# Two transposes of Wq issued ahead of the transpose of tile 7's normalised rows

## The chip, the cores and the metric

The kernel runs on one core of one Trainium2 chip. The metric is device time in microseconds (us), as a median of runs; one further execution is recorded by the hardware profiler, and all times inside the kernel are counted from the start of that record's span.

## What is computed

The reference is one transformer layer on 2048 rows of 640 numbers in bf16: linear attention with 32 heads of 20 features, whose feature map is a pair of softmaxes, and then a feed-forward part with silu.

```python
qkv = layernorm(x) @ wqkv                     # to q, k, v, each 32 heads x 20
pq, pk = q @ w_phi, k @ w_phi                 # per head, 20 x 20
phi_q = concat(softmax(pq), softmax(-pq))     # 40 features; phi_k likewise
kv = phi_k^T @ v;  z = sum_s(phi_k)           # per head
o = (phi_q @ kv) / (phi_q . z + 1e-6)
h = x + o @ wo
out = h + silu(layernorm(h) @ w1) @ w2
```

## The kernel before

The 2048 rows are 16 tiles of 128 rows. The small matrices w_phi are folded into the weights first: Wfk is Wk times w_phi, Wfq is Wq times w_phi, so that each tile is projected straight onto the arguments of the softmaxes. Matmuls contract over the partitions, in five chunks of 128.

**One list sets the order.** Every step of the program has a short name, and the list `ORDER` (lines 18 to 55) writes them out in the order in which their instructions are emitted. Each engine carries out its own instructions in that order; only semaphores hold it against the other engines. A step that only issues DMAs is an instruction of SyncE (SP), which has its own queue and takes its issues strictly in turn: an issue that waits for its data holds all the issues behind it.

The names that matter here, with t for a tile and r for one of six blocks of Wq:

- `st`t, `rs`t, `xn`t: mean and variance of tile t (VectorE, L432 and L433), one over the deviation (L441 and L444 on GpSimd, or L438 and L439 on ScalarE), and the normalised rows (L448; on GpSimd for most tiles from 3 on). `xn` has four buffers.
- `xt`t: the transpose of the normalised rows into XnT. From tile 4 on it is a DMA transpose issued by SyncE (L477). It reads what `xn`t has written.
- `K`t, `V`t: the projections of tile t onto keys and values, ten matmuls each (L496), with XnT as the stationary operand. `Q`t is the same for queries (L534).
- `wq`r: block r of the columns of Wq, 120 wide, read from DRAM and transposed into WTq by a DMA transpose on SyncE (L386). It waits for no other step.
- `fq`r, `fq`r`e`: five matmuls that fold block r (L398), and ScalarE's copy of the result into Wfq (L404). The blocks are folded in the order 2, 3, 0, 1, 4, 5. `Q0` needs all six.
- `ex`t, `su`t, `rk`t, `sc`t: the exponentials of tile t's keys (ScalarE, L551), their sums (VectorE, L555), the inverse of the sums (ScalarE, L563 and L564) and the scaling (VectorE, L568). `kv`t are the eleven matmuls that add the tile to the sum over all rows (L587), and `ve`t copies the values out of PSUM (L572).
- `load`i: a load of a later weight (L488), issued by SyncE. `load6` brings the first three chunks of w2.
- Later: `D`, `E`, `ot`, `G` for the attention's second half, `hn`, `ht` for the second normalisation and its transposes to HnT (L769), `u` and `d` for the feed-forward part (L824, L864).

PSUM is used in three pairs of banks, taken in turn: `fq0`, `K6`, `fq1`, `K7`, `V6`, `fq4` and so on, each pair to be read out before its next use.

The two lines that issue the transposes in question are these:

```python
nc.sync.dma_start_transpose(WTq[:, r : r + 1, :], A_wqkv[:, at : at + P])      # wq, L386
nc.sync.dma_start_transpose(xt(t), xn_.pop(t)[:])                              # xt, L477
```

Of the kernel before, what the change touches and what calls it, by code (L numbers as in the profile page):

```python
# [22 lines left out]
rs4 xt2 K1 ex0 V0.2 ones5 xn4 wq4 V0.3 V0.1 st5 x2 wph0 su0 ex1 su1 rs5 V0.4 K2 xn5 phq xt3 V1 rs6 ex2  # L23
V2 x3 st7 xn6 rk0 X8 su2 rs7 ve1 ve2 ve0 xt4 sc0 st8 V3 fq2 xt5 rk2 ve3 K3 xn7 st11 ones3 fq2e V4 K4 rk1
ex3 wq3 ones2 ve4 kv0 ones6 sc1 ones7 sc2 V5 fq3 rs8 st9 ex4 su3 st10 rs9 wq0 kv1 ve5 ones4 xt6 su4 K5
fq0 fq3e K6 rk3 ex5 xt7 kv2 wq1 wq5 fq1 fq0e sc3 ex6 K7 load6 su5 fq1e mask kv3 ex7 xn8 st13 V6 xt8
mask0 rk4 ve6 rk5 su6 sc4 rs11 fq4 fq4e xn9 zeros st12 V7 ve7 rk6 V8 rs10 sc5 xt9 xn10 load3 V9 su7 ve8
fq5 rs12 rs13 st14 ve9 xt10 kv4 fq5e rk7 load7 K8 ex8 sc6 kv5 st15 xn11 K9 su8 xn12 sc7 Q0 kv6 K10 xt11
kv7 ex9 Q1 rk8 rs15 load2 su9 xn13 qe0 ex10 qe1 K11 xt13 sc8 rs14 mask1 rk9 qs0 kv8 xt12 xn14 load11 V10
# [911 lines left out]
```

## Time and profile before

| | |
|---|---|
| median of three runs | 237.27 us (236.63 to 237.54) |
| the profiled execution's own time | 236.82 us |
| its span | 234.8 us |
| TensorE (PE) busy | 229.5 us, 98% of the span |
| VectorE (DVE) busy | 165.8 us, 71% |
| ScalarE (ACT) busy | 105.1 us, 45% |
| GpSimd (POOL) busy | 64.4 us, 27% |
| granted TensorE clock | 0.999 |

The profile has a page with sums by engine and by line, and the trace behind it can be asked for stretches of time: a timeline by engine (start, duration, what ran), who waited for whom (total, times, longest), and the chain of work that ended last (start, duration, what). DMA transposes appear in SyncE's rows with the time that their issue takes; the time to landing is told beside them. Names such as `XnT<-xn` say what is written from what.

### The profile page before, as it was taken

How to read it: one execution, taken by the hardware profiler on the slowest of the kernel's cores; microseconds unless marked ns; L12 is line 12 of the kernel's file. 1: busy time of each engine (PE TensorE's matmuls, PEld its weight loads, DVE VectorE, ACT ScalarE, POOL GpSimd, SP SyncE). 2: the span in 40 equal slices, each digit the busy share in tenths (PEclk: the TensorE clock that was granted, in tenths of full speed). 3: DMA queues.
4: the chain of work that ended last, by engine and by line, in shares of the span. 5: the costliest groups of instructions: out<-in, count | busy, mean ns of one | idle time of the engine just before them, and what ended most of it. 6: DMA issues, size and time to landing. Idle time of an engine off the chain costs nothing.

```text
span 234.8 us, 5031 instructions
## 1 busy us (share of the span) xinstructions
PE 229.5 (98%) x1984; PEld 161.2 (69%) x1984; DVE 165.8 (71%) x349; ACT 105.1 (45%) x222; POOL 64.4 (27%) x103
## 2 busy tenths in 40 slices
PE   8999989999999999999999999999999999999995
PEld 6777767777777777887545777645677455778874
DVE  3999979999999999999999795792472330404031
ACT  3999979877969754610234100054300326001410
POOL 5699999996000020121010111011020010100000
PEclk9999999999999999999999999999999999999999
DMA  6995379668976749694325946127313301011011
GB/s 165 346 228 138 88 162 149 181 59 172 245 270 73 155 94 159 148 120 95 81 64 133 163 97 173 31 56 176 72 24 88 98 0 28 30 29 56 8 56 56
DMA packets 67213, 26.79 MB, mean 114 GB/s; under 512 B 60151, under 2 KB 66167, under 8 KB 67063
## 3 DMA queue, kind: packets, MB, share of 16 engines
q1 hardware_dynamic: 66535, 26.47, 52.9%
q8 instruction: 15, 0.25, 0.5%
q10 hardware_dynamic: 656, 0.03, 0.2%
q14 instruction: 7, 0.06, 0.1%
HBM read 9.64 MB, written 2.62 MB: 52 GB/s over the span
## 4 chain that ended last, share of the span: by engine, by line
PE 87%; DVE 5%; DMA 3%; ACT 2%; issue 1%; POOL 1%; SPq 0%; DVEq 0%; POOLq 0%
PE banks L864 24%; PE banks L824 24%; PE banks L496 16%; PE banks L742 7%; PE banks L534 4%; PE banks L587 2%; PE banks L215 2%; PE banks L867 2%; PE banks L709 2%; DMA HnT<-xn 2%; DMA WTq<-in_A_wqkv_dram 1%; DVE Sq L660 1%; ACT Wfk L323 1%; PE banks L835 1%; DVE O L722 1%
## 5 line engine op out<-in xcount | busy, mean ns | idle before, releaser
L844 ACT ACTIVATE shT<-banks 128x512 bf16<-128x512 f32 (+1 forms) x53 | 28.7, 591 | 83.2 <-PE banks L824 83.2
L864 PE MATMUL banks<-w_sb,shT 128*128 128x320 bf16 (+2 forms) x429 | 61.3, 295 | 0.0
L824 PE MATMUL banks<-HnT,w_sb 128*128 128x512 bf16 (+1 forms) x325 | 59.0, 336 | 0.5 <-DMA HnT<-xn 0.5
L864 PEld LDWEIGHTS <-shT 128*128 128x128 bf16 x429 | 41.1, 98 | 15.2
L824 PEld LDWEIGHTS <-w_sb 128*128 128x128 bf16 x325 | 31.1, 98 | 22.8 <-issue 0.6
L441 POOL TENSOR_SCALAR rs<-mv 128x1 f32<-128x1 f32 x26 | 7.7, 298 | 137.1 <-DVE mv L433 136.9
L873 DVE TENSOR_TENSOR o_t<-banks,X 128x320 bf16<-128x320 f32 (+2 forms) x33 | 14.9, 474 | 39.6 <-PE banks L867 26.7
L496 PEld LDWEIGHTS <-XnT 128*128 128x128 bf16 x300 | 28.2, 98 | 10.5 <-DMA XnT<-xn 0.4
L448 POOL TENSOR_SCALAR xn<-X,mv,rs 128x640 bf16<-128x640 bf16 x12 | 31.0, 2586 | 0.4
L432 DVE BATCH_NORM_STATS2 st<-X 128x6 f32<-128x320 bf16 x64 | 27.9, 477 | 3.3 <-DMA X<-in_A_x_dram 3.2
L656 ACT ACTIVATE EQ<-banks 128x360 bf16<-128x360 f32 (+2 forms) x52 | 22.0, 514 | 8.4 <-PE banks L534 8.2
L742 PE MATMUL banks<-wo_sb,OT 128*128 128x320 bf16 x160 | 24.8, 299 | 0.0
L660 DVE TENSOR_REDUCE Sq<-EQ 128x66 f32<-128x1320 bf16 x16 | 24.1, 1517 | 0.0
L534 PE MATMUL banks<-Wfq,XnT 128*128 128x360 bf16 (+2 forms) x160 | 23.5, 299 | 0.0
L749 DVE TENSOR_TENSOR X<-banks,X 128x320 bf16<-128x320 f32 x32 | 14.5, 483 | 12.6 <-PE banks L742 12.5
L555 DVE TENSOR_REDUCE Sk<-EK 128x64 f32<-128x1280 bf16 x16 | 23.3, 1464 | 0.2
L551 ACT ACTIVATE EK<-banks 128x640 bf16<-128x640 f32 x32 | 20.8, 701 | 4.4 <-PE banks L496 2.0
L496 PE MATMUL banks<-Wfk,XnT 128*128 128x320 bf16 x150 | 22.5, 299 | 0.0
L496 PE MATMUL banks<-Wv,XnT 128*128 128x320 bf16 x150 | 21.8, 299 | 0.0
L742 PEld LDWEIGHTS <-OT 128*128 128x128 bf16 x160 | 15.1, 98 | 6.5
L534 PEld LDWEIGHTS <-XnT 128*128 128x128 bf16 x160 | 15.1, 97 | 6.2
L444 POOL TENSOR_TENSOR rs<-rs,nhalf_t 128x1 f32<-128x1 f32 x26 | 15.9, 613 | 2.2
(71 smaller groups left out, 203.9 us busy)
## 6 DMA issues: line engine op xcount, KB each, us to landing
out_dram<-o_t SPq DMA_DIRECT2D x15, 160.0 KB, 2.0
w_sb<-in_B_w_dram SPq DMA_DIRECT2D x5, 432.0 KB, 3.9
w_sb<-in_B_w_dram SPq DMA_DIRECT2D x3, 480.0 KB, 4.5
X<-in_A_x_dram SPq DMA_DIRECT2D x1, 1280.0 KB, 7.3
Wk<-in_A_wqkv_dram SPq DMA_DIRECT2D x5, 160.0 KB, 3.5
Wv<-in_A_wqkv_dram SPq DMA_DIRECT2D x5, 160.0 KB, 5.7
wo_sb<-in_A_wo_dram SPq DMA_DIRECT2D x1, 800.0 KB, 5.7
X<-in_A_x_dram SPq DMA_DIRECT2D x1, 640.0 KB, 5.9
```

Source lines behind the costliest of these rows:

```text
L432: nc.vector.bn_stats(st[:, i, :], X[:, t, i * HD : (i + 1) * HD])
L448: eng.tensor_scalar(out=xn_[t][:], in0=X[:, t, :], scalar1=mv_.pop(t)[:, 0:1], scalar2=rs_.pop(t)[:], op0=ALU.subtract, op1=ALU.mult,)
L496: nc.tensor.matmul(ps[:, g, 0:HD], XnT[:, c, t * P : (t + 1) * P], W[:, c, g * HD : (g + 1) * HD], start=(c == 0), stop=(c == C - 1),)
L534: nc.tensor.matmul(ps[:, 0 : e - a], XnT[:, c, t * P : (t + 1) * P], Wfq[:, c, a:e], start=(c == 0), stop=(c == C - 1),)
L551: nc.scalar.activation(E5[:, :, :, b, :], p4, AF.Exp, scale=sign)
L555: nc.vector.tensor_reduce(sk[t][:], ek[t][:, 0 : H * HF].rearrange("p (q f) -> p q f", f=DH), axis=AX.X, op=ALU.add)
L656: nc.scalar.activation(features(t, a, b)[:, :, :, i], p4, AF.Exp, scale=sign)
L660: nc.vector.tensor_reduce(sq[t][:], EQ[0][:, t, :, 0:FCH].rearrange("p c (q f) -> p c q f", f=DH), axis=AX.X, op=ALU.add)
L742: nc.tensor.matmul(ps[:, 0:HD], ot[t][:, c, :], wo_sb[:, c, g * HD : (g + 1) * HD], start=(c == 0), stop=(c == C - 1),)
L824: nc.tensor.matmul(ps[:, at : at + n], w1_sb[:, c, fc * P : fc * P + P], HnT[u][:, c, 0:n], start=(c == 0), stop=(c == C - 1),)
L844: nc.scalar.activation(shT[u][:, f0 * n : f1 * n], ps_of.pop(("u", u, f0))[:, 0 : (f1 - f0) * n], AF.Silu)
L864: nc.tensor.matmul(ps[:, 0 : b - a], shT[u][:, at : at + P], w2_sb[:, fc, a:b], start=(fc == 0), stop=False,)
```

## The change

Two names of the list move: `wq1` and `wq5` stand ahead of `xt7` and `kv2`, in place of behind them.

```diff
-fq0 fq3e K6 rk3 ex5 xt7 kv2 wq1 wq5 fq1 fq0e sc3 ex6 K7 load6 su5 fq1e mask kv3 ex7 xn8 st13 V6 xt8
+fq0 fq3e K6 rk3 ex5 wq1 wq5 xt7 kv2 fq1 fq0e sc3 ex6 K7 load6 su5 fq1e mask kv3 ex7 xn8 st13 V6 xt8
```

`xt7`, `wq1` and `wq5` are issues of SyncE; `kv2` belongs to PE. SyncE's issues in this stretch were xt6, xt7, wq1, wq5, load6, xt8, and are now xt6, wq1, wq5, xt7, load6, xt8. The instructions of the other four engines, and their order, are the same as before.

## The prediction

> **What bounds the kernel now.** The page comes first: PE is busy 229.5 of 234.8 us, so at most 5.3 us are to be had, and a saving counts only where PE stands still. The chain of waits from 28 to 36.6 us then shows the place that the change touches.
>
> ```profile
> 28.51 2.91 DMA WTq<-in_A_wqkv_dram
> 31.42 0.05 issue
> 31.47 0.44 PE banks L398 x5
> 31.90 1.36 PE banks L496 x10
> ```
>
> The fold of query block 1 (fq1, five matmuls, L398) starts when the second block of Wq (wq1, L386) has landed, 2.91 us after its issue. The waits between 24 and 44 us give the price, and what hangs on it:
>
> ```profile
> DVE EK L568 <- ACT Rk L564: 1.7, 1, 1.7
> ...
> PE banks L398 <- DMA WTq<-in_A_wqkv_dram: 1.0, 1, 1.0
> ```
>
> PE is idle 1.04 us (30.43 to 31.47). K7 behind it is late by as much, so are ex7 and rk4 on ACT, and DVE stands 1.67 us before sc4 (L568, 35.45). From there DVE has no gap over 0.2 us until 110. The only other PE gap over 0.1 us after 11 us is 0.52 us before L824 at 92.73. SyncE's timeline says why wq1 is late:
>
> ```profile
> 23.48 4.98 SPq L477 DMA_TRANSPOSE XnT<-xn  x2
> 28.51 2.58 SPq L386 DMA_TRANSPOSE WTq<-in_A_wqkv_dram  x2
> 31.14 0.58 SPq L488 DMA_DIRECT2D w_sb<-in_B_w_dram  x1
> 31.82 3.45 SPq L477 DMA_TRANSPOSE XnT<-xn  x2
> ```
>
> The first row holds xt6 (23.48 to 24.70) and xt7 (27.25 to 28.46). Between them SyncE stands 2.55 us, until GpSimd has written xn7 (24.70 + 2.52 = 27.22), and wq1 and wq5 queue behind it though their data lie in DRAM.
>
> **The change part by part.** Nothing is added or removed. Three issues change places on SyncE; kv2, also named in the moved stretch, is PE's and keeps its place there.
>
> (1) *wq1 and wq5, earlier.* An issue takes 1.26 us and the next follows 0.05 later: wq1 24.75 to 26.01, wq5 26.06 to 27.32. The six wq took 2.9 to 6.4 us to land, wq1 itself 2.91: it lands near 27.7, at 29.0 with the 4.3 us of xt6 ahead of it. fq1 is ready for it at 30.43. The wait goes: **-1.04 us** at fq1, with 1.4 us of cover.
>
> (2) *xt7, moved past.* It issues at 27.37 in place of 27.25 and landed 3.5 us after issue, at 30.76; now 30.87 or so. K7 is the next on PE and, without the wait, is ready at 30.43 + 0.43 = 30.86. So xt7 is next late, by 0 to 0.1: I take 0.06, and keep **-0.97**. Bounds from the twelve xt: the fastest (2.4 us) lands before 30 and costs nothing; xt6, which also followed two wq at once, took 4.3: 31.63, and K7 is where it was. I take xt7's own row.
>
> (3) *Moved with it.* load6 (480 KB) issues at 28.6, not 31.14. xt8 stood behind it; it now waits for xn8 alone (GpSimd, 30.86), issues 0.9 us earlier and lands by 35.7 (issue end 32.1 plus the 3.5 it took before). V8 comes at 36.58 - 0.97 = 35.61: nothing lost. xt9 still goes at 34.05 and landed at 37.06, V9 wants it at 37.0: nothing to 0.1.
>
> (4) *The earlier PE then meets GpSimd.* GpSimd works without a break from 10.9 to 54 us, and each xt goes when its xn is done. V13 is the close one: xt13 issued at 47.88 and landed at 50.30 (2.4 us); V13 started at 50.86, the second ten of these thirty:
>
> ```profile
> 49.34 4.24 PE L496 MATMUL banks<-Wv,XnT 128*128 128x320 bf16 x30
> ```
>
> With PE 0.97 earlier V13 wants it at 49.89. GpSimd gains something: its small steps are long where they start while DVE runs an L568.
>
> ```profile
> 44.03 0.23 POOL L441 TENSOR_SCALAR rs<-mv 128x1 f32<-128x1 f32 x1
> 44.35 1.00 POOL L444 TENSOR_TENSOR rs<-rs,nhalf_t 128x1 f32<-128x1 f32 x1
> 45.35 2.51 POOL L448 TENSOR_SCALAR xn<-X,mv,rs 128x640 bf16<-128x640 bf16 x1
> ```
>
> That L444 started inside the L568 at 44.11 to 44.92 and took 1.00, not the usual 0.57; the L441 at 37.53 took 0.89, not 0.24. With DVE 0.97 earlier both stand clear: 0.43 + 0.65 saved, less up to 0.45 where xn10 now starts inside sc4, and 0.06 to 0.3 where xn12 and rs13 meet sc7. I take 0.37 to 0.56, so xn13 ends near 47.4, and xt13 would land near 49.85: in time. From 64 us DVE hangs on PE again (0.13 us of idle before su15, for ex15), so the 0.97 reaches the HnT gap at 92.73 and the end.
>
> The Trainium skill's page "SBUF — State Buffer", section "SBUF: two separate sides", calls the port pair of VectorE and GpSimd an exclusive lock held by whichever starts first. The rows above agree (1.00 against 0.57); without that rule xt13 would land at 50.30 as before, and the saving would end at 0.45.
>
> (5) *But a transfer of another kind goes by PE's clock.* Queue q8 moves 16 KB of instructions at a time, and each comes after some 250 more PE instructions in the trace (217, 432, 684, 946 before the first four), so it will be as much earlier as PE. The DMA view from 50.1 to 50.3 shows the fourth (start 50.19, 1.70 us long), and in the same answer the xt12 issued beside it:
>
> ```profile
> q8 instruction: 1, 0.02, 53.1%
> ...
> XnT<-xn SPq DMA_TRANSPOSE x1, 4.3
> ```
>
> xt12 took 4.3 us instead of 2.4. The second fetch (25.35, 1.23 us) fell on the last packets of xt6: 15 of its 16 completions came by 26.05, the last at 27.75, 1.17 us after the fetch ended. In before, xt13's last packets started at 49.85, so the fetch missed it by 0.34 us. Now PE, and the fetch with it, is 0.97 earlier and xt13 only 0.37 to 0.56: the fetch moves 0.41 to 0.60 towards it, and falls on its last packets. Price: fetch at 49.22, over at 50.50 (1.28, the two others of 1.23 and 1.28 before 40 us), xt13 complete 1.17 later at 51.67, V13 at 51.72 where it was at 50.86: **+0.86 us** against before. Bounds: a fetch of 1.23 and a completion 0.55 after it, as the undisturbed ones have, give +0.2; 1.70 long gives +1.28. If the fetch misses, -0.97.
>
> The fetches are also where the skill speaks against my sum: "Runtime: NRT & Kernel Launch", section "Instruction fetch mechanics", says that the cost of crossing a 16 KiB boundary is mostly hidden. By it the sum would stay at -0.97. xt12's 4.3 us, against 2.4, is why I weigh it lower: the fetch may cost the engine that it feeds nothing, and still hold up a transfer of another queue.
>
> K12 behind it has xt12 in time in either case (52.5, wanted after 52.9), and nothing later takes the +0.86 back: ex12 and su12 had 0.17 us of room, and DVE then reaches su15 by PE's clock.
>
> *Sum:* -1.04 at fq1, +0.07 for xt7, +1.83 at V13 = +0.86. The profiled execution took 236.82 (span 234.8 and 2.0 around it), so 237.68 by it. The median of before is 237.27, 0.45 above that execution; set on the median, **238.1**.
>
> **The rivals.**
> - *The gain is carried through*: the fetch misses xt13. For it: the margin that decides is 0.1 us of last packets, and one engine of sixteen carries the fetch. -0.97, 236.3; with less of the 0.52 at 92.73, 235.9.
> - *Half is kept*: xt7 lands some tenths later, or GpSimd gains nothing and V13 waits for an xt13 that lands at 50.30 undisturbed. PE is then at most 0.5 early. -0.45, 236.8.
> - *Slower at once*: K7 waits for xt7 behind wq5. The point from which it decides is a landing after 31.7. For it: the xt6 row (4.3 us behind two wq); against it: SyncE's issues are as far apart (1.3) as the wq landings (1.5), so no backlog should build. At 4.3 us there is nothing left to gain (237.3); at 2.4 us behind a wq5 that lands at 31 it is 33.4, +1.6: 238.9.
>
> That the change doesn't do what it says is excluded: only SyncE's order differs between the two programs.
>
> **How the numbers follow.** Fetch on xt13: 0.44 (half of it above +1.18, with a long fetch or more of xt13 caught). Carried through: 0.30 (0.16 of it beyond -1.18, since the three runs scatter by 0.9 and the 92.73 gap can shrink). Half kept: 0.12. xt7 late: 0.14 (0.08 above +1.18). 0.5% is 1.19 us, about what a measurement of this kernel can tell from no change: faster 0.16, same 0.54, slower 0.30. The likeliest case alone spans 237.5 to 238.6; with the gains and the late xt7, 235.9 to 238.9.
>
> **What would show it.** Right: no gap before fq1; K7 near 30.9; xn13 done before 47.6; a q8 transfer near 49.2 with xt13 landing after 51; a PE gap of 1 to 2 us before V13. Wrong: xt13 landing before 50 with no gap (then the end is 0.9 to 1.0 earlier), or K7 behind its old 31.74. The forecast fails if the fetches do not move with PE, or if a fetch leaves a transfer that is all but done alone.

## The result and the profile after

The changed kernel takes 238.61 us (median of 22 runs, 236.86 to 239.31) against 237.28 us before (22 runs, 236.63 to 238.43). The ratio is 1.0043, with a 95% interval of 1.0027 to 1.0059: 1.0 us slower (0.6 to 1.4). The two medians alone lie 1.33 us apart. Of the 22 runs of each kernel, 17 lie above 237.9 us after the change and 3 before it.

The profiled execution took 239.23 us (span 237.2, where before's was 234.8). SyncE's timeline has the new order:

```profile
23.91 1.22 SPq L477 DMA_TRANSPOSE XnT<-xn  x1
25.18 3.38 SPq L386 DMA_TRANSPOSE WTq<-in_A_wqkv_dram  x2
28.65 1.22 SPq L477 DMA_TRANSPOSE XnT<-xn  x1
29.92 0.58 SPq L488 DMA_DIRECT2D w_sb<-in_B_w_dram  x1
31.33 1.22 SPq L477 DMA_TRANSPOSE XnT<-xn  x1
```

The rows are xt6, wq1 and wq5 together, xt7, load6, xt8. wq1 is early, but the pair takes 3.38 us and not 2.58, so xt7 goes at 28.65. This execution was about 0.4 us behind before's already where the two programs do not differ (xt6 at 23.91 against 23.48); beyond that xt7 is 1.0 us later.

PE's timeline around the two places where it now stands still (the bracket is the idle time before the row and what ended it):

```profile
30.66 0.42 PE L398 MATMUL banks<-phi_q,WTq 128*128 128x120 bf16 x5
32.28 1.53 PE L496 MATMUL banks<-Wfk,XnT 128*128 128x320 bf16 x10 [1.19 <-DMA XnT<-xn]
...
49.67 1.52 PE L496 MATMUL banks<-Wv,XnT 128*128 128x320 bf16 x10
52.60 2.62 PE L496 MATMUL banks<-Wv,XnT 128*128 128x320 bf16 x18 [1.41 <-DMA XnT<-xn]
```

fq1 (L398) waits no more. K7 right behind it waits 1.19 us for xt7: the 1.04 us before fq1 have changed their name. The second gap is new: V13 waits 1.41 us for xt13. The chain of waits goes back through that transfer to GpSimd:

```profile
44.48 0.88 POOL rs L441
45.36 0.07 issue
45.43 0.57 POOL rs L444
46.00 2.50 POOL xn L448
48.50 0.03 POOL rs L441
48.53 4.02 DMA XnT<-xn
52.55 0.05 issue
52.60 0.45 PE banks L496 x2
```

Before, xt13 landed 2.42 us after its issue; here it took 4.02. Its 16 completions came at 50.79 to 50.95 for fifteen of them and at 52.55 for the last. The DMA view of the stretch from 50.4 to 50.6 shows what started there:

```profile
q8 instruction: 1, 0.02, 29.1%
q1 hardware_dynamic: 27, 0.00, 7.2%
```

This is PE's instruction fetch of 16 KB (start 50.51), and the 27 small packets are the last of xt13.

The difference of 2.4 us between the two spans can be followed by the times at which PE starts the same matmul: 0.4 at the start (gaps at 5 to 10 us, on loads that the change does not touch), 0.15 at fq1 and K7 together, 0.2 won back at V8 (which in before started at 36.62 for an xt8 that landed at 36.58), 1.57 at V13 (1.41 of it counted as idle, because PE's rows overlap), and 0.5 more in the gap before L824 (1.02 against 0.52).

### The profile page after: what moved, and what is told of

Its sections match the earlier page's. It is cut to its first block, busy times and chain, and to the rows that moved or that the text cites. A ratio compares the mean times of both kernels' runs of the same rounds, so it can differ in the third digit from the quotient of the medians.

```text
span 237.2 us, 5031 instructions
## 1 busy us (share of the span) xinstructions
PE 229.0 (97%) x1984; PEld 160.5 (68%) x1984; DVE 165.9 (70%) x349; ACT 104.9 (44%) x222; POOL 64.7 (27%) x103
## 4 chain that ended last, share of the span: by engine, by line
PE 69%; POOL 13%; DVE 6%; DMA 5%; issue 5%; SPq 1%; POOLq 0%; DVEq 0%
PE banks L864 24%; PE banks L824 24%; POOL xn L448 8%; PE banks L742 7%; PE banks L496 5%; PE banks L534 3%; PE banks L867 2%; DMA Wk<-in_A_wqkv_dram 2%; DMA XnT<-xn 2%; PE banks L709 2%; POOL rs L444 2%; DMA HnT<-xn 1%; POOL rs L441 1%; DVE Sq L660 1%; PE banks L587 1%
## 5 line engine op out<-in xcount | busy, mean ns | idle before, releaser
L824 PE MATMUL banks<-HnT,w_sb 128*128 128x512 bf16 (+1 forms) x325 | 59.0, 336 | 1.0 <-DMA HnT<-xn 1.0
L824 PEld LDWEIGHTS <-w_sb 128*128 128x128 bf16 x325 | 31.2, 98 | 23.2 <-issue 1.1
L441 POOL TENSOR_SCALAR rs<-mv 128x1 f32<-128x1 f32 x26 | 8.3, 320 | 139.2 <-DVE mv L433 139.0
L722 DVE TENSOR_TENSOR O<-banks,Rd 128x360 bf16<-128x360 f32 (+1 forms) x32 | 15.7, 491 | 1.1
```

The costliest lines, as they stand in the source:

```text
L824: nc.tensor.matmul(ps[:, at : at + n], w1_sb[:, c, fc * P : fc * P + P], HnT[u][:, c, 0:n], start=(c == 0), stop=(c == C - 1),)
```

## The experiments

Three theories stood against one another. **A**: the loss is the stall before V13, made by an instruction fetch that falls on the last packets of xt13. **B**: the loss is K7's wait for xt7 behind two blocks of Wq. **C**: xt13 is late through GpSimd or other transfers, and the fetch is only beside it.

### One block at a time

```diff
 # w1_only                              # w5_only
-ex5 xt7 kv2 wq1 wq5 fq1               -ex5 xt7 kv2 wq1 wq5 fq1
+ex5 wq1 xt7 kv2 wq5 fq1               +ex5 wq5 xt7 kv2 wq1 fq1
```

> Only wq1 stands ahead of xt7; wq5 stays behind it. Theory A (an instruction fetch of PE falls on the last packets of xt13, and the stall before V13 is the loss): wq1 fits into SyncE's pause, xt7 issues as in before, the gap before fq1 goes and K7 waits 0 to 0.3 us. PE is then 0.7 to 1.0 us early, and the fetch near 50.2 us with it, so it falls on xt13 more fully: a gap of 1 to 2.5 us before V13, and in the end -0.2 to +1.2 us against before. Theory B (the loss is K7 waiting for xt7 behind two blocks of Wq): with xt7 in time the 1.04 us are kept, -0.9 to -1.0 us against before, and V13 has no gap.

> Only wq5 stands ahead of xt7; wq1 stays behind it. Theory A: xt7 issues within 0.2 us of before, wq1 too, the gap before fq1 is 1.0 to 1.3 us, PE and the fetch keep their places, so the time is that of before to 0.4 us. Theory B: xt7 lands later behind wq5 and wq1 behind both: +0.5 to +1.0 us.

w1_only: 237.25 us against 237.35, ratio 1.0009 (0.9981 to 1.0037). w5_only: 237.13 us, 0.9989 (0.9963 to 1.0016). The profile of w1_only, PE's two gaps:

```profile
31.24 1.53 PE L496 MATMUL banks<-Wfk,XnT 128*128 128x320 bf16 x10 [0.50 <-DMA XnT<-xn]
...
51.44 1.80 PE L496 MATMUL banks<-Wv,XnT 128*128 128x320 bf16 x12 [1.28 <-DMA XnT<-xn]
```

With wq1 alone in SyncE's pause, half of the wait is saved (0.50 before K7, where before had 1.04 before fq1; theory A had expected at most 0.3), and V13 takes 1.28 back. B foretold -0.9 to -1.0 and no gap at V13, so B is wrong as the whole of it. w5_only keeps before's time, as A said; but its profiled execution (238.24 us, its second longest of twelve) has the gap before V13 too, 1.32 us, with PE not early. So the stall does not need PE to be early: a few tenths in either direction decide.

### Taking the stall away from the changed kernel, in two ways

The first way lets V13 come after V11, so that PE wants xt13 1.36 us later. The second leaves out five warming matmuls near 4.7 us; the fetches, which come by the count of PE's instructions, then fall ten instructions later.

```diff
 # after_v11_first                      # after_less_warm
-V10 V13 ... V11 ... ve13 ve10 ve11    -wk2 warm15 warm16 warm17 warm18 warm19 WK3
+V10 V11 ... V13 ... ve11 ve10 ve13    +wk2 WK3
```

> The changed kernel with V11 ahead of V13 (and ScalarE's copies of the two likewise): PE wants xt13 1.36 us later. Theory A: xt13 may land as late as 52.5 and the gap before V13 falls from 1.4 us to 0 to 0.3; the time is 1.0 to 1.4 us below the changed kernel, that is, before's to 0.4 us. Theory B: K7's wait is untouched, the time stays that of the changed kernel, +1.0 us against before.

> The changed kernel without five of the twenty warming matmuls near 4.7 us, where PE waits for Wk in any case: 10 instructions fewer ahead of every fetch, so each fetch comes 10 PE instructions later, some 0.7 us near V10. The arithmetic of the outputs is the same. Theory A: the fetch near 50.5 moves to 51.2 and misses xt13 (its last packets start by 51.0); no gap before V13, and the time is 1.0 to 1.4 us below the changed kernel. Theory B, and a theory C that xt13 is late through GpSimd or other transfers: the same time as the changed kernel, +1.0 us against before.

after_v11_first: 237.35 us, 0.9994 of before (0.9976 to 1.0012). after_less_warm: 237.21 us, 1.0001 (0.998 to 1.0023). Both are back at before's time, by two edits of different kinds: the one gives V13 room, the other moves the fetch. In after_less_warm 4 of the 12 runs still lie above 237.9 us (238.17 to 238.62); no profile shows why. PE's waits from 24 to 60 us in after_less_warm are one line:

```profile
PE banks L496 <- DMA XnT<-xn: 1.7, 1, 1.7
```

That is K7, 1.73 us before 32.14, longer than in the changed kernel. Theory B has nothing left here: the wait it blames is there in full, and the loss is gone. after_v11_first has 1.62 us before K7 and likewise no gap at V13. In its profiled execution xt13 landed 2.41 us after issue, so that profile does not show the stall being covered; only the times do (all 12 runs at or below 237.86, where 17 of 22 of the changed kernel's were above 237.9).

### Making the stall without the change

```diff
 # before_more_instr: SyncE's old order
-wk2 warm15 ... warm19 WK3     # 5 matmuls, 256 columns
+wk2 warm15 ... warm24 WK3     # 10 matmuls, 128 columns
```

> The kernel before, with SyncE's old order, but ten warming matmuls of half the width in place of the last five of full width: the same PE time, 10 PE instructions more ahead of every fetch, so the fetch near 50.2 us comes some 0.7 us earlier, at 49.5, while xt13's packets still run (49.0 to 49.85). Theory A: xt13 lands 1 to 2 us later, V13 has a gap of 0.8 to 2 us, and the loss appears without the change: +0.6 to +1.4 us against before. Theory C (xt13 late through GpSimd or other transfers): nothing changes, within 0.4 us of before.

237.38 us, ratio 1.0001 (0.9974 to 1.0027): the median did not move, and so far the expectation failed. The profiled execution, 238.05 us, has the stall:

```profile
51.77 1.53 PE L496 MATMUL banks<-Wv,XnT 128*128 128x320 bf16 x10 [0.94 <-DMA XnT<-xn]
```

The fetch came at 49.63, 0.56 earlier than in before, and xt13's last completion at 51.72 where the other fifteen were in by 50.24. The stall can be had without the change, but the median says that most of the executions did not have it (3 of 12 lie above 237.9 us).

### Removing K7's wait: the blocks issued far ahead

SyncE pauses from 12.5 to 18.2 us. Issued there, behind X8, the two blocks are out of everyone's way.

```diff
 # early
-rk0 X8 su2            -ex5 xt7 kv2 wq1 wq5 fq1
+rk0 X8 wq1 wq5 su2    +ex5 xt7 kv2 fq1
 # early_v11_first: with V11 ahead of V13 as above
 # early_v11_xt12: and xt12 ahead of xt13 on SyncE
-K11 xt13 sc8 rs14 mask1 rk9 qs0 kv8 xt12
+K11 xt12 xt13 sc8 rs14 mask1 rk9 qs0 kv8
```

> wq1 and wq5 are issued right behind X8, in SyncE's pause before xt4 (12.5 to 18.2 us); xt6 and xt7 stand as in before with nothing between them. No gap before fq1, 0 to 0.2 us before K7: PE is about 1.0 us early. Theory A: V13 then meets with xt13, which lands at 50.3 at best and at 51 to 52 if the fetch, as much earlier as PE, falls on it: a gap of 0.5 to 2.3 us there, and -0.5 to +1.0 us against before in the end. Theory B (only SyncE's order around xt7 counts): -0.9 to -1.1 us.

> As the last, with V11 ahead of V13 (and ScalarE's copies likewise), which gives xt13 1.36 us more. Theory A: most of the gain is kept, -0.5 to -1.0 us against before; what is next late is xt12 ahead of K12, up to 0.5 us. Theory B: the same as without the exchange.

> As the last, with xt12 issued ahead of xt13 as well: xn12 is done at 44.1 us and xt12 waited behind xt13 only in SyncE's order. K12 then has xt12 by 47, and a fetch near 49 to 50 us finds xt13 alone, with 1.4 us of room. No PE gap over 0.2 us between 31 and 60 us; -0.9 to -1.4 us against before by theory A.

early: 237.69 us, ratio 1.001 (0.9988 to 1.0032). There is no gap before fq1 and 0.12 before K7; kv8, just ahead of V10 and V13, starts 0.74 us earlier than in before (48.26 against 49.00) though xt6 had been issued 0.66 later, and all of it goes at V13:

```profile
51.53 1.67 PE L496 MATMUL banks<-Wv,XnT 128*128 128x320 bf16 x11 [1.41 <-DMA XnT<-xn]
```

early_v11_first: 236.31 us, 0.9954 (0.9931 to 0.9977), no PE gap over 0.2 us from 11 to 91 us. In its profile xt13 took 3.93 us, hit by the fetch as in early, and V11 covered it: here the cover is seen. early_v11_xt12: 236.24 us, 0.9954 (0.9929 to 0.9978): xt12 ahead adds nothing, and its profiled execution (236.72 us) still has 0.63 us before K7, where xt7 took 3.57 us to land, and 0.45 before V13, where xt13 took 4.43. The expected absence of gaps did not come.

### The same with the fetch moved, and three controls

```diff
 # early_less_warm: the early blocks, V13 in its old place, warm15 to warm19 left out
 # before_v11_first: before, V11 ahead of V13
 # after_again, before_again: unchanged, for a second profile
```

> wq1 and wq5 behind X8 as before, V13 in its old place, and five warming matmuls fewer, so that each fetch comes 10 PE instructions later (some 0.7 us). Theory A: the fetch near 49.4 us moves to 50.1 and misses xt13, which then lands 2.4 us after its issue, near 50; V13 waits 0 to 0.5 us for it. The 1.41 us gap goes, and the time is 0.5 to 1.0 us below before. If something else made xt13 late: as with the earlier place alone, +0.4 us.

> The kernel before with V11 ahead of V13, a control for that exchange. Theory A: most executions of before miss the stall, so the median falls by 0 to 0.3 us only; the long executions (over 237.9 us, 4 of the 22 first ones) become rarer. If the exchange is worth 1 us by itself, the earlier reading of it was wrong.

> The changed kernel once more, for a second profile beside the first. Theory A: if this execution is among the longer ones (238.2 us and more), it has a gap of 1.2 to 1.6 us before V13 and an xt13 that lands 3.9 us or more after its issue; if it is near 237.4 us, there is no such gap. In both a gap of 1.0 to 1.7 us before K7. The median stays 0.6 to 1.4 us above before's.

> The kernel before once more, for a second profile. Theory A: at its usual 236.9 to 237.5 us a gap of 1.0 to 1.3 us before fq1, none before V13, xt13 landing about 2.4 us after issue; at 238 us and more the gap before V13 is there too. The same time as before.

early_less_warm: **235.75 us, ratio 0.9948 (0.9928 to 0.9969)**, 1.2 us below before, a little more than the 0.5 to 1.0 expected; this beats both kernels. PE's waits from 24 to 60 us are empty; of SyncE's transposes issued at 47.1 us, the trace tells:

```profile
L477 SPq DMA_TRANSPOSE XnT<-xn x1: 1207/1207/1207, 47.1 to 47.1; - x1
...
DMA to landing us min/median/max: 2.4/2.4/2.4
```

xt13 lands after 2.4 us, as in before, and in early it took 4.0; the fetch starts at 51.25 and no longer at 49.44, later by more than the 0.7 expected. The same SyncE order and the same PE order after the first 5 us: only the count of instructions ahead differs. Of the 2.0 us between the two profiled spans (235.8 and 233.8), 1.5 arise at V13 and 0.4 ahead of it, most of that before fq1. What five matmuls fewer are worth by themselves is not known, because before was not run without them; the profiles put the main part at V13.

before_v11_first: 237.42 us, 1.0022 (0.9996 to 1.0049). The exchange by itself is worth nothing, so its effect above was the stall's. The long executions did not become rarer as expected (5 of 12 above 237.9; of before's first 22 it was three, not the four that the expectation counts). The profiled one, 238.88 us, has a gap of 2.03 us at 11 us, on the load of Wv, and none at V13; behind the gap, from 12.3 to 15.7 us, the granted clock is 0.50, which makes 0.993 over the whole span. Three of the other four (239.30 to 239.41) have the same 0.993 and the rest of the twelve 0.999 or 1.000, so those three were probably long for the same reason and not by the stall; the fifth, 238.02, is not explained. Without the four at 0.993 the median of the other eight is 237.35, before's own.

after_again: 238.33 us (7 runs), 1.0047 (1.0029 to 1.0066). Its profiled execution was the shortest of the seven, 237.70 us: 1.59 us before K7, no gap before V13, xt13 landed in 2.41 us. before_again: 237.18 us, 0.9996 (0.9981 to 1.0012), profiled 237.12 us: 1.66 us before fq1. So the second pair of profiles, without the stall in either, shows the exchange of the two waits (1.59 for 1.66) at nothing: PE starts V10 at 49.90 in both. The 0.6 us by which this execution of the changed kernel is still longer lie in the gap before L824, 0.88 against 0.24.

### All profiles in one table

The room is the time from the end of xt13's issue on SyncE to the start of the fetch.

```
kernel               room us   xt13 issue to landing us
before_more_instr     0.57       3.87
early_v11_first       0.63       3.93
w1_only               0.68       3.90
w5_only               0.68       3.94
early_v11_xt12        0.72       4.43
after                 0.77       4.02
early                 0.78       4.02
after_again           1.08       2.41
after_v11_first       1.08       2.41
before                1.10       2.42
before_again          1.12       2.41
before_v11_first      2.91       2.40
early_less_warm       2.95       2.43
after_less_warm       2.96       2.42
```

The landings fall into two groups, 2.4 and 3.9 to 4.4 us, with an edge between a room of 0.78 and 1.08. The transposes xt6 and xt10 of the same fourteen profiles fall into the same two groups wherever a 16 KB fetch starts behind them: thirteen with a room of 0.54 to 0.83 us landed after 4.0 to 4.3 us, four with 1.08 to 1.28 after 2.4 to 2.5. Theory C would need the landing to follow something else; early and early_less_warm have the same SyncE order and an xt13 issued 0.37 us apart, and lie at opposite ends. The kernel before stands at 1.10, a few hundredths to three tenths from the edge.

## Why the prediction was right or wrong

**The outcome** was foretold: slower, 238.1 us, from the likeliest case (the fetch on xt13); measured 238.61. The route to it was right in its second half and wrong in the first, so that the number came out partly by luck.

1. *wq1 lands in time for fq1*: right. It landed at 28.38, wanted at 30.66.
2. *xt7 next late, by 0.06*: this term was mis-sized, 1.19 us of idle before K7 in the profile (1.59 to 1.73 in three other profiles of this order). The prediction gave each wq an issue of 1.26 us and counted on the pair filling SyncE's pause exactly. But PE's second fetch (25.77) ran while wq1 was being issued, and that issue took 2.06 us. So wq5 ended at 28.55, xt7 issued 1.28 later than foreseen (0.4 of it the start), and fifteen of its completions were in by 31.63, the last, with an 8 KB fetch started at 30.90, at 32.23. The rival "K7 waits for xt7" had the right place; its cause was not a backlog of transfers but a longer issue. The 4.3 us of xt6, which the prediction counts in that rival's favour, belonged to the fetch and not to the two wq ahead: in after_less_warm and early_less_warm, where the fetch starts 1.1 us after the end of xt6's issue, it lands in 2.46 us behind the same two. A smaller error lies in the reading of PE's rows, which overlap: K7 starts 0.27 us after fq1 (31.47 and 31.74), though fq1's row is 0.44 long. By the starts (kv2 at 29.93, fq1 0.34 behind it, K7 0.27 behind that) K7 was ready at 30.54 and not at 30.86, so even an xt7 that landed at 30.87 would have been 0.3 to 0.4 late. early, which takes both blocks out of the pause, shows the term by itself: K7's gap falls to 0.12.
3. *load6 and xt8*: right, no gap at V8 or V9.
4. *PE 0.97 us early at V13*: wrong, as it follows from 2; PE was 0.3 us later there, no more than this execution's late start. *GpSimd 0.4 to 0.6 faster*: not in this kernel, where rs13 started inside the L568 (0.90 + 0.57 us, in place of 0.23 + 1.00). The reason behind it held where its condition was met: in early, with DVE ahead, the two steps took 0.32 + 0.57.
5. *The fetch falls on xt13's last packets*: right in place, kind and nearly in size. One completion in sixteen, 1.6 us after the others; a gap of 1.41 us against the 1.83 forecast. What brought them together in this kernel was not PE's 0.97 but three tenths: xn13 came 0.64 later and the fetch 0.32. The route that was forecast, with PE early, is seen in early: PE was 0.74 early at kv8, xt13 landed at 51.48 and V13 started at 51.53, where 51.67 and 51.72 were forecast. (In before V13 started at 50.70 by the starts of V10's matmuls, 0.136 us apart from 49.34 on, and not at 50.86; the forecast price was 0.16 too low for that.) Taking the fetch away (after_less_warm), or the need for xt13 (after_v11_first), takes the loss away.
6. *Sum*: -0.97 + 1.83 = +0.86 was forecast; in the profiled execution it was +0.15 and +1.41 of idle time, beside the 0.4 at the start and the 0.5 before L824, for which there was no term; the medians differ by 1.33. The first term was off by 1.1 us, the second by 0.4 the other way. That 238.1 still came within 0.5 us of 238.61 was luck: the stall, which the prediction made depend on an early PE, came without one.

"Half is kept" and "carried through" did not occur in this kernel; the second is what early_less_warm shows (0.9948).

The Trainium skill's page "Runtime: NRT & Kernel Launch", section "Instruction fetch mechanics", calls the cost of a block boundary mostly hidden. For PE's own stream the traces agree: no PE gap is put down to a fetch. What a fetch does to a DMA transpose that is under way is not covered by that sentence; there 2.4 us became 3.9 to 4.4.

**Still open.** By their times about three in four executions of the changed kernel are hit (one of its two profiles shows it). Why so many, when SyncE and PE stand near V13 almost as in before, was not settled. The room in the two unhit profiles of the changed and the old order is the same (1.08 and 1.10), so the share may come from tenths in GpSimd's steps beside DVE's L568, which differ from one profile to the next; this is not shown. w5_only and before_more_instr have the stall in their profiles and not in their medians. The gap before L824 was larger after the change in both pairs of profiles (1.02 against 0.52, 0.88 against 0.24) and was not tried by itself, so up to half a microsecond of the loss may lie there; before_more_instr and early have 0.66 and 0.63 too, so it is not the change's alone.

## What to carry to other kernels

A wait that is removed is worth only the slack of what stands next on the same engine: here the transpose that was moved past had almost none, and the order cost about what it saved. Put a load without inputs into a pause that is longer than it, not into one that it fills to the hundredth. And when a change that should be free costs a microsecond, look at how many of the sixteen completions of the late transfer were on time: one missing points to something else that held a small part of the transfer back, here an instruction fetch, and a few instructions more or less far ahead can move it.

## What the runs showed of the hardware

- A fetch of 16 KB for PE (0.9 to 1.8 us in these profiles near 50 us) started 0.57 to 0.78 us after the end of xt13's issue went with one of its sixteen completions being 1.5 to 2.0 us behind the others, and with a landing after 3.9 to 4.4 us in place of 2.4 (seven profiles of seven); at 1.08 us and more the landing took 2.4 (seven of seven). xt6 and xt10 show the same landings (in two of their thirteen late ones all sixteen completions were late).
- A fetch that starts 0.5 to 0.8 us into a transpose's issue on SyncE lengthens that issue, to 1.9 to 2.7 us in all sixteen cases among the xt and wq of these profiles: wq1's took 2.06 us beside the fetch at 25.77 (after), 2.42 us beside that at 25.49 (w1_only), against 1.26 us alone. Everything behind it on SyncE is later by the difference. Where the fetch started 1.03 to 1.07 us into xt12's issue (before, before_again, after_again, after_v11_first), the issue kept its 1.26 us, and all sixteen completions came late instead: xt12 landed after 4.3 us, against 2.5 without a fetch near it (early_less_warm).
- Ten PE instructions taken out at 5 us moved the fetch near 50 us by 1.2 to 1.8 us (50.51 to 51.70 in the changed order, 49.44 to 51.25 in early), more than the 0.7 us that they take there, and brought the changed kernel from 1.0043 to 1.0001 of before.
